# Attention and gated-MLP backward on one core: one late gradient store split 17/15/96 over the DMA engines, and small loads behind the last eight stores

## The chip, the cores and the metric

The kernel runs on one core of a Trainium2 chip. The metric is device time in microseconds (us) for one execution of the whole program; lower is better. Five engines run beside each other and wait for each other through semaphores: TensorE (PE) multiplies matrices, VectorE (DVE) and ScalarE (ACT) do elementwise work, GpSimd (POOL) and SyncE (SP) mainly start transfers here. Sixteen DMA engines move the data between HBM and the core's on-chip memory (SBUF). A transfer (a "DMA") is started by SP, by ACT or by Pool; each of the three has its own queue, and a transfer is cut into packets that are shared out over some or all of the sixteen engines. When all of a transfer's engines have finished, its completion semaphore stands 16 higher.

## The reference, cut to what matters

One decode step (one token) of a block with cached attention and a SwiGLU MLP in parallel, forward and backward:

```
xn  = layernorm(x)                                        # x: 1 x 1 x 640
q   = (xn @ wq) as 32 heads of 128                        # wq: 640 x 4096
p   = softmax(q . k_cache * 128**-0.5)                    # k_cache, v_cache: 32 heads x 8192 x 128
att = concat(p @ v_cache) @ wo                            # wo: 4096 x 640
mlp = (silu(xn @ w1) * (xn @ w3)) @ w2                    # w1, w3: 640 x 1728, w2: 1728 x 640
out = x + att + mlp
grads = vjp(out)(grad_out)   # of x, k_cache, v_cache, wq, wo, w1, w3, w2
```

All tensors are bf16. With one token, every weight gradient is an outer product: wo's gradient, for instance, is the attention output (4096 values) times grad_out (640 values). The gradients of the two caches are as large as the caches: for each head 8192 x 128 values of V's gradient (p times a row) and as many of K's. So the program reads each cache once and writes two tensors of their size: 151.34 MB in and 151.34 MB out.

## The kernel before

The program first does the MLP with its gradients, then goes head by head through the 32 heads. For each head SP loads K (2 MB) and V (2 MB). DVE multiplies them by the query and by the output gradient, PE sums, DVE and ACT build the two gradients of the head in the SBUF tile `ot`, and a store writes each out. Up to head 29 these stores go to Pool's queue, one of 2 MB each (`outer_v`, line 458). The last two heads (`TAIL = 2`) store each gradient in two halves of 1 MB from SP instead (line 456): eight stores, called s1 to s8 below, issued when DVE and ACT have finished the half.

The heads come in eight groups of four (`GH = 4`, `NG = 8`). `finish_steps` ends a group: ACT writes the group's wo gradient over the tile `wo_g` (line 374), and stores it (128 rows, one per SBUF partition, of 2560 values or 5,120 bytes). For group 6 (`g == NG - 2`) the store isn't issued there but put on the list `late` (lines 375 and 376). In head 29's turn (`h == H - 3`) the list is emptied on Pool's queue (line 787), behind Pool's last 2 MB store: wq's gradient of a pair of groups (1,280 KB), wo's gradient of group 6 (640 KB), wq's gradient of group 6 (640 KB). Behind the list stands `turn_lanes(0)`, explained next. Then, after the last head, SP stores wo's gradient of group 7 (line 827), ACT stores wq's of group 7 (`dwq_t`, line 824, forty pieces of 1,024 bytes for each DMA engine), SP stores x's gradient (`dx_bf`, line 855) and ACT stores the output (`fin_bf`, five rows of 256 bytes, line 860).

Some helpers count DMA engines, which the kernel calls lanes (`LANES = 16`). The kernel's count goes like this: a Pool transfer of 128 rows gives each engine eight rows; a Pool transfer whose number of rows has no factor of 16 goes to as many neighbouring engines as the largest factor up to 16 says (120 rows to 15 engines, 15 rows to 15, 11 rows to 11, and 17 rows, a prime, to one), starting at the engine behind the one where the last such transfer ended. `dealt[0]` holds that starting engine, and `turn_lanes(to)` moves it to `to` by loading a few rows of 32 bytes into a tile that nobody reads (`lane_pad`): k rows move it by k, and 17 rows by one. `sparing` uses this to keep 120 of 128 rows of some wq stores off engine 4 (`SPARED`). `turn_lanes(0)` at the end brings the count back to 0, with 11 rows on engines 5 to 15.

The order of instructions on each engine is the order of the program text (`manual_schedule`). The compiled program gives the transfers of SP and ACT eight completion semaphores in turn, and Pool's transfers another eight. A transfer that takes over a semaphore waits, on its issuing engine, until the transfer that had it before has landed. So each transfer of SP or ACT waits for the one eight before it in their common order.

Of the kernel before, what the change touches and what calls it, by code (L numbers as in the profile page):

```python
# [16 lines left out]
P = 128  # L17
# [4 lines left out]
def kernel(  # L22
# [22 lines left out]
    nc = tc.nc  # L45
# [23 lines left out]
    LANES = 16  # L69
# [23 lines left out]
    wq_v = A_wq.rearrange("(p ci) n -> p ci n", ci=NC)  # L93
    dwq_v = out_4.rearrange("(p ci) n -> p ci n", ci=NC)
    wo_v = A_wo.rearrange("(g p r) c -> g p r c", p=P, r=GH)
    dwo_v = out_5.rearrange("(g p r) c -> g p r c", p=P, r=GH)
# [7 lines left out]
    with tc.manual_schedule(engines=ORDERED):  # L104
# [26 lines left out]
        lane_pad = consts.tile([P, 2, 2, 8], BF16, name="lane_pad")  # L131
        dealt = [0, 0]

        def turn_lanes(to):
            k = (to - dealt[0]) % LANES
            if k:
                rows = k if k > 1 else LANES + 1
                nc.gpsimd.dma_start(lane_pad[0:rows, dealt[1] % 2], wq_v[0:rows, 0:2, 0:8])
                dealt[:] = to % LANES, dealt[1] + 1

        def deal(dst, src, p0, p1):
            nc.gpsimd.dma_start(dst[p0:p1], src[p0:p1])
            dealt[0] = (dealt[0] + (LANES - 1 if p0 == 0 else P - p0)) % LANES

        def sparing(dst, src):
            rows = P - P % (LANES - 1)
            if dealt[0] == (SPARED + 1 + P - rows) % LANES:
                deal(dst, src, rows, P)
                deal(dst, src, 0, rows)
                turn_lanes(SPARED + 1)  # L150
            else:
                turn_lanes(SPARED + 1)
                deal(dst, src, 0, rows)
                turn_lanes(SPARED + 1)
                deal(dst, src, rows, P)

        def store(dst, src, later=False, by=nc.gpsimd.dma_start):
            if later:
                late.append((by, dst, src))
            else:  # L160
                by(dst, src)
# [5 lines left out]
        def wq_part(b, c0, n):  # L167
            cols = slice(b * GW * DH, (b + 1) * GW * DH)
            return wq_two[:, c0:c0 + n, b % 2, :], wq_v[:, c0:c0 + n, cols], dwq_v[:, c0:c0 + n, cols]
# [180 lines left out]
        def on_cols(g):  # L350
            on_ps = ps_w.tile([P, GH], F32, name="on_ps", tag="w")
            for hh in range(GH):
                nc.tensor.matmul(on_ps[hh * (P // GH):(hh + 1) * (P // GH), :], lhsT=sel[:], rhs=grp[g]["om"][:, hh, :],
                                 start=True, stop=True, skip_group_check=True)
            on = small.tile([P, GH], F32, name="on")
            nc.scalar.copy(on[:], on_ps[:])
            on_bf = small.tile([P, GH], BF16, name="on_bf")
            nc.scalar.copy(on_bf[:], on[:])
            return on, on_bf
# [6 lines left out]
        def finish_steps(g):  # L366
            G_ = grp[g]
            wo_g = G_["wo"]
            on, on_bf = on_cols(g)
            behind_o.append((g, on_bf))  # L370
            yield
            assert not behind_o
            for r in range(GH):
                nc.scalar.activation(wo_g[:, r, :], g_bc_bf[:], ACTF.Copy, scale=on[:, r:r + 1])
            if g == NG - 2:
                store(dwo_v[g], wo_g[:], True)
            else:
                nc.scalar.dma_start(dwo_v[g], wo_g[:])
            yield
            yield  # L380
            b, k = divmod(g, HB)
            for ci in range(NC):
                nc.scalar.activation(G_["wq"][:, ci, :], G_["dqbc"][:].rearrange("p h d -> p (h d)"),
                                     ACTF.Copy, scale=xn_col[:, ci:ci + 1])
            if g < NG - HB and k == HB - 1:
                if g == NG - HB - 1:
                    part, _, dst = wq_part(b, 0, NC)
                    store(dst, part, True)
                else:
                    columns.extend((b, *part) for part in WQ_PARTS)  # L390
                    store_columns()
            if g >= NG - HB:
                store(dwq_v[:, :, g * GH * DH:(g + 1) * GH * DH], G_["wq"], True)
            grp.pop(g)
# [38 lines left out]
        def outer(st, vec, w2, wf, which, h, half):  # L433
            outer_v(st, vec, w2, which, h, half, outer_s(st, vec, wf, half))
# [14 lines left out]
        def outer_v(st, vec, w2, which, h, half, n):  # L449
            j0 = half * JH  # L450
            nc.vector.tensor_tensor(st.ot[half][:, 0:n],  # L451
                                    vec.rearrange("p (a b) -> p a b", b=2).unsqueeze(1).to_broadcast([P, n, DH // 2, 2]),
                                    w2[:, j0:j0 + n, :].unsqueeze(2).to_broadcast([P, n, DH // 2, 2]), ALU.mult)
            dst = {"V": dvc, "K": dkc}[which][h]
            if h >= H - TAIL:
                nc.sync.dma_start(dst[:, j0:j0 + JH, :], st.ot[half].rearrange("p j a b -> p j (a b)"))
            elif half:
                nc.gpsimd.dma_start(dst.rearrange("p j d -> p (j d)"), st.rows[:])  # L458
                if columns:
                    store_columns()  # L460
# [4 lines left out]
        def store_columns():  # L465
            b, c0, n = columns.pop(0)
            part, _, dst = wq_part(b, c0, n)
            store(dst, part, by=sparing)
# [96 lines left out]
        def keep_dq(st):  # L565
            G_, hh = st.G, st.hh
            if hh == 0:
                G_["dqbc"] = wpool.tile([P, GH, DH], BF16, name="dqbc_g", tag="dqbc_g", bufs=1)
            nc.scalar.copy(G_["dqbc"][:, hh, :], st.ps_db)
            if hh == GH - 1 and st.g < NG - 1:  # L570
                steps.append(finish_steps(st.g))
# [109 lines left out]
        for b in range(NB):  # L681
            rows, src = (P, w2t[:, b, :]) if b < NF else (REST, w2r)
# [62 lines left out]
        for h in range(H - 1):  # L745
            n = new_head(h + 1) if h + 1 < H else None
            c = hs.pop(h)
            g, hh = divmod(h, GH)
# [51 lines left out]
        g = c.g  # L800
# [33 lines left out]
        for ci in range(NC):  # L834
            k, c = divmod(ci * P, WIDE_COLS)
# [55 lines left out]
```

## Time and profile before

| | us |
|---|---|
| median of 3 runs | 718.69 (718.24 to 719.10) |
| the profiled execution, its own time | 718.87 |
| its span in the profile | 717.1 |
| granted TensorE clock, mean | 0.889 |
| busy: PE, DVE, ACT, POOL | 557.1, 630.6, 484.2, 49.5 |
| mean rate of all transfers | 423 GB/s |

The times of the runs are those of the device for one execution. The profile is of one execution: its span runs from the first to the last instruction, and 1.8 us of its own time lie outside the span. "Busy" counts computing instructions alone, so it doesn't hold the time in which an engine waits. The share of the DMA engines is the mean over the sixteen. The profile's packet records name the queue, start, duration and size of each packet, but not the DMA engine that moved it.

### The profile page before, as it was taken

What the parts mean: (1) busy time and instruction counts of PE and PEld (TensorE: products, weight loads), DVE (VectorE), ACT (ScalarE), POOL (GpSimd) and SP (SyncE); (2) the same over time, 40 slices, a digit from 0 to 9 for tenths busy, and PEclk for the clock granted to TensorE, in tenths of its full rate; (3) what the DMA queues carried; (4) which work ended last, traced back from release to release, by engine and by line L of the source; (5) the groups of instructions that cost most, each with busy time, mean ns of one, the idle gap of its engine ahead of it and who ended that gap; (6) DMA issues with size and microseconds to landing.
All of it is one profiled execution on the core that took longest, in us unless ns stands there. A gap on an engine that the chain in (4) does not pass through costs nothing.

```text
span 717.1 us, 9854 instructions
## 1 busy us (share of the span) xinstructions
PE 557.1 (78%) x3516; PEld 272.4 (38%) x3516; DVE 630.6 (88%) x723; ACT 484.2 (68%) x1472; POOL 49.5 (7%) x91
## 2 busy tenths in 40 slices
PE   6878988878788777776887787488868789877772
PEld 4753443334333333333343344143434334333331
DVE  5789999999989895997899899499999889899982
ACT  1275778796769656694587867468677857777552
POOL 0010000000001110000000110000000000000100
PEclk9698999998989998997899989899999878999995
DMA  9999999999999999999999999999999999999997
GB/s 364 416 425 430 431 430 430 429 429 429 428 432 428 426 428 424 429 427 426 432 431 428 430 422 426 428 430 429 428 428 431 429 430 431 429 430 429 429 421 288
DMA packets 27039, 303.32 MB, mean 423 GB/s; under 512 B 3249, under 2 KB 3959, under 8 KB 9327
## 3 DMA queue, kind: packets, MB, share of 16 engines
q1 hardware_dynamic: 12832, 154.88, 50.9%
q0 software_dynamic: 10960, 137.72, 45.2%
q10 hardware_dynamic: 3198, 10.10, 3.5%
q8 instruction: 27, 0.44, 0.2%
q14 instruction: 22, 0.17, 0.1%
HBM read 151.34 MB, written 151.34 MB: 422 GB/s over the span
## 4 chain that ended last, share of the span: by engine, by line
DMA 45%; DVE 31%; PE 17%; ACT 3%; issue 2%; POOL 0%; ACTq 0%; DVEq 0%; POOLq 0%
DMA Kt<-in_A_k_cache_dram 28%; DVE T L425 15%; DMA out_dram<-ot 12%; DVE ot L451 10%; PE ob L500 4%; DMA lane_pad<-in_A_wq_dram 4%; PE psS L427 3%; PE psDP L427 3%; ACT ot L445 2%; DVE DP_sb L526 1%; DVE S_sb L472 1%; PE dh_ps L591 1%; PE dx_ps L626 1%; PE gate_ps L602 1%; PE ps_od L516 1%
## 5 line engine op out<-in xcount | busy, mean ns | idle before, releaser
L427 PE MATMUL psDP<-T,ident_bf 128*128 128x512 bf16 x512 | 157.0, 462 | 64.6 <-DVE T L425 64.6
L427 PEld LDWEIGHTS <-ident_bf 128*128 128x128 bf16 x1024 | 108.3, 109 | 212.6 <-issue 140.1
L445 ACT ACTIVATE ot<-qs_g,Uf 128x128 bf16<-128x128 bf16 x504 | 154.0, 394 | 45.1 <-DVE Uf L539 27.2
L425 DVE TENSOR_TENSOR T<-Kt,qs_g 128x4096 bf16<-128x4096 bf16 x64 | 146.4, 2287 | 20.0 <-DMA Kt<-in_A_k_cache_dram 18.8
L445 ACT ACTIVATE ot<-do_g,Pf 128x128 bf16<-128x128 bf16 x512 | 156.3, 389 | 6.2 <-DMA out_dram<-ot 5.2
L425 DVE TENSOR_TENSOR T<-Vt,do_g 128x4096 bf16<-128x4096 bf16 x64 | 146.0, 2282 | 3.9 <-DMA Vt<-in_A_v_cache_dram 3.9
L427 PE MATMUL psS<-T,ident_bf 128*128 128x512 bf16 x512 | 129.0, 397 | 17.7 <-DVE T L425 17.7
L451 DVE TENSOR_TENSOR ot<-qs_g,U 128x3072 bf16<-128x3072 bf16 (+2 forms) x64 | 112.6, 1760 | 11.9 <-DMA out_dram<-ot 11.8
L451 DVE TENSOR_TENSOR ot<-do_g,P 128x3072 bf16<-128x3072 bf16 (+2 forms) x64 | 112.3, 1755 | 6.3 <-DMA out_dram<-ot 5.2
L458 POOL DMA_DIRECT2D out_dram<-ot x60 | 32.2, 537 | 549.2 <-DVE Uf L539 303.6
L500 PE MATMUL ob<-Vt,P 128*4 128x512 bf16 x512 | 64.1, 394 | 0.0
L500 PE MATMUL ob<-Kt,U 128*4 128x512 bf16 x512 | 60.5, 379 | 1.4 <-DVE U L533 1.4
L494 ACT ACTIVATE Pf<-E,rZ 128x16 f32<-128x16 f32 (+1 forms) x32 | 9.8, 307 | 60.2 <-DVE rZ L489 60.2
L558 ACT ACTIVATE dq_diag<-ident_bf,odq 128x128 bf16<-128x128 bf16 x32 | 12.8, 401 | 47.8 <-DVE odq L554 47.8
L516 PEld LDWEIGHTS ps_od<-pick,wide 128*128 128x128 f32 x256 | 38.1, 213 | 7.8 <-issue 3.0
L516 PE MATMUL ps_od<-pick,wide 128*128 128x2 f32 x256 | 33.8, 254 | 0.5 <-ACT wide L508 0.5
L500 PEld LDWEIGHTS <-U 128*4 128x4 bf16 x512 | 19.8, 84 | 37.5 <-DVE U L533 6.6
L476 PE MATMUL sm<-ident_f,mrow 128*128 128x128 f32 x64 | 15.9, 331 | 22.3 <-DVE mrow L474 22.3
L500 PEld LDWEIGHTS <-P 128*4 128x4 bf16 x512 | 20.8, 86 | 25.8 <-issue 3.5
L508 ACT COPY wide<-ob 128x256 f32<-128x256 f32 x64 | 20.1, 363 | 12.7 <-PE ob L500 12.7
L472 DVE TENSOR_REDUCE S_sb<-psS 128x64 f32<-128x512 f32 x32 | 21.9, 685 | 5.6 <-PE psS L427 5.6
L317 ACT COPY woT<-ps_t 128x512 bf16<-128x512 bf16 x40 | 22.9, 577 | 4.2 <-PE ps_t L312 3.6
(174 smaller groups left out, 552.4 us busy)
## 6 DMA issues: line engine op xcount, KB each, us to landing
out_dram<-ot POOLq DMA_DIRECT2D x60, 2048.0 KB, 24.4
Kt<-in_A_k_cache_dram SPq DMA_DIRECT2D x32, 2048.0 KB, 26.6
Vt<-in_A_v_cache_dram SPq DMA_DIRECT2D x32, 2048.0 KB, 20.0
out_dram<-ot SPq DMA_DIRECT2D x8, 1024.0 KB, 12.7
out_dram<-wo_g ACTq DMA_DIRECT2D x6, 640.0 KB, 15.1
wo_g<-in_A_wo_dram ACTq DMA_DIRECT2D x6, 640.0 KB, 15.8
wq_two<-in_A_wq_dram SPq DMA_DIRECT2D x1, 2560.0 KB, 23.8
w1t<-in_B_w_dram SPq DMA_DIRECT2D x1, 2160.0 KB
```

The costliest lines, as they stand in the source:

```text
L317: nc.scalar.copy(woT[:], ps_t[:])
L425: nc.vector.tensor_tensor(T[:], src[:, :, ds_], vec[:, ds_].unsqueeze(1).to_broadcast([P, J, DHH]), ALU.mult)
L427: nc.tensor.matmul(ps[:], lhsT=ident_bf[:], rhs=T[:, :, RUN * i:RUN * (i + 1)], start=(half == 0 and i == 0), stop=(half == 1 and i == DHH ...
L445: nc.scalar.activation(st.ot[half][:, JH - n + j].rearrange("p a b -> p (a b)"), vec, ACTF.Copy, scale=wf[:, half, j:j + 1])
L451: nc.vector.tensor_tensor(st.ot[half][:, 0:n], vec.rearrange("p (a b) -> p a b", b=2).unsqueeze(1).to_broadcast([P, n, DH // 2, 2]), w2[:, ...
L458: nc.gpsimd.dma_start(dst.rearrange("p j d -> p (j d)"), st.rows[:])
L472: nc.vector.tensor_reduce(st.S[:], st.ps["S"][:], AX.X, ALU.add)
L476: nc.tensor.matmul(st.sm[:, 8:8 + P], lhsT=mrow[:].to_broadcast([P, P]), rhs=ident_f[:], start=True, stop=True, skip_group_check=True)
L500: nc.tensor.matmul(ob[c0:c0 + WIDE, :], lhsT=w2[:, WIDE * q:WIDE * (q + 1), 0], rhs=src[:, WIDE * q:WIDE * (q + 1), :].rearrange("p j d -> ...
L508: nc.scalar.copy(part[:], ob[:, i * (WIDE // 2) * DH:(i + 1) * (WIDE // 2) * DH])
L516: nc.tensor.matmul(st.od, lhsT=st.wide[i][:, b * DH:(b + 1) * DH], rhs=pick[:, r, :], start=(r == 0), stop=(r == WIDE - 1), skip_group_che ...
L558: nc.scalar.activation(dq_diag[:], ident_bf[:], ACTF.Copy, scale=odq[:, 1:2])
```

## The change

Two things change; no arithmetic does.

First, Pool's late store of wo's gradient of group 6 becomes three stores, through the new function `more_to_last`: `turn_lanes(15)` first (10 rows, from engine 5 to engine 14), then 17 rows (one engine, by the kernel's count engine 15), 15 rows (engines 0 to 14) and 96 rows (six for each engine). By this count engine 15 moves 23 rows of 5,120 bytes where it moved 8, and each other engine 7. The final `turn_lanes(0)` now starts at engine 15, so it loads 17 rows where it loaded 11.

Second, `mark()` follows each of the eight half stores of the last two heads. It loads k rows of 16 bytes from wq into rows of `lane_pad` that nothing else uses: 17, 10, 9, 8, 7, 6 and 4 rows behind s1 to s7, and 3 and then 2 rows behind s8. They are nine loads on SP's queue.

```diff
+        def more_to_last(dst, src):
+
+            turn_lanes(LANES - 1)
+            r0 = 0
+            for k in (LANES + 1, LANES - 1, P - 2 * LANES):
+                nc.gpsimd.dma_start(dst[r0:r0 + k], src[r0:r0 + k])
+                r0 += k
+            dealt[0] = LANES - 1
+
+
+        marks = [(17,), (10,), (9,), (8,), (7,), (6,), (4,), (3, 2)]
+        marked = [24]
+
+        def mark():
+            for k in marks.pop(0):
+                nc.sync.dma_start(lane_pad[marked[0]:marked[0] + k, 0, 0], wq_v[0:k, 0, 0:8])
+                marked[0] += k
+
...
             if g == NG - 2:
-                store(dwo_v[g], wo_g[:], True)
+                store(dwo_v[g], wo_g[:], True, by=more_to_last)
...
             if h >= H - TAIL:
                 nc.sync.dma_start(dst[:, j0:j0 + JH, :], st.ot[half].rearrange("p j a b -> p j (a b)"))
+                mark()
```

In the compiled program PE, DVE and ACT have the same instructions in the same order. Pool has 3 transfers more and SP 9. Since the semaphores go round in turn, the partners of the waits change: s5, s6 and s7 now wait for s1, s2 and s3; the mark behind s7 waits for s4 to have landed; the two behind s8 wait for the mark behind s5 and for s6; the wo store of group 7 (old line 827) waits for the mark behind s6; the `dx_bf` store for s7; the `dwq_t` store for the mark behind s3, and the `fin_bf` store for s5. Before, the wo store waited for s3, the `dx_bf` store for s4, `dwq_t` for s1 and `fin_bf` for s2.

## The prediction

> **What bounds the kernel now.** I read the page's head first, then its chain of waits, then a table of windows over the last ten microseconds, then SP's waits at the end, and last the trace's packet records.
>
> ```profile
> span 717.1 us, 9854 instructions
> DMA  9999999999999999999999999999999999999997
> HBM read 151.34 MB, written 151.34 MB: 422 GB/s over the span
> DMA 45%; DVE 31%; PE 17%; ACT 3%; issue 2%; POOL 0%; ACTq 0%; DVEq 0%; POOLq 0%
> ```
>
> The sixteen DMA engines are busy in 39 of 40 slices, and transfers are the largest part of the chain. The change touches nothing before 667 us, so only the end matters. The windows there (columns: PE, PEld, DVE, ACT, POOL busy, clock, DMA share, GB/s):
>
> ```profile
> 707.00:708.00 1.00, 0.00 (x0) 0.00 (x0) 0.49 (x3) 0.00 (x0) 0.00 (x0) 0.50 1.04 414
> 709.00:710.00 1.00, 0.00 (x0) 0.00 (x0) 0.00 (x0) 0.00 (x0) 0.00 (x0) 0.50 0.74 293
> 711.00:712.00 1.00, 0.00 (x0) 0.00 (x0) 0.00 (x0) 0.00 (x0) 0.00 (x0) 0.50 0.70 261
> 713.00:714.00 1.00, 0.00 (x0) 0.00 (x0) 0.00 (x0) 0.00 (x0) 0.00 (x0) 0.50 0.31 107
> 715.00:716.00 1.00, 0.00 (x0) 0.00 (x0) 0.00 (x0) 0.00 (x0) 0.00 (x0) 0.50 0.01 1
> ```
>
> ```profile
> SPq L886 <- DMA out_dram<-ot: 5.2, 2, 2.8
> SPq L886 <- DMA out_dram<-dwq_t: 2.7, 1, 2.7
> ```
>
> Computing ends by 708 us. What is left is transfers, and SP waits for their landing at the program's end (the two waits). The DMA share falls in steps: the engines don't run out together. The last one sets the end, so the question is which engine gets the 15 extra rows.
>
> The records don't name engines, but they can be chained: a packet's successor on its engine starts 3 or 4 ns before its recorded end (of 1,157 Pool packets of 16,384 bytes after 600 us, 1,089 have a start exactly 4 ns before their end; ties are settled by the number of packets that each transfer has per engine). The last increments of the semaphores, and the last Pool load's packets, show the spread (us):
>
> ```
> dwq_t, 16 engines: 708.72 708.79 709.00 709.01 710.01 | 711.96 712.86 713.08 713.27 713.39 713.76 | 714.95 715.21 715.37 715.56 715.87
> fin_bf, engines 0-4: 709.08 710.25 713.45 715.12 716.05
> last lane_pad load, start on engines with a row (5-15): 695.34 695.45 697.17 | 702.00 702.09 702.39 702.43 702.80 | 704.68 705.59 705.69
> the five engines without a row (0-4): 693.89 695.60 703.36 706.07 706.32
> ```
>
> So five engines are early, six are in the middle, five are late, and of engines 5 to 15 three, five and three. The last of all is one of 0 to 4: `fin_bf` lands there at 716.05, and the span ends 1.05 later.
>
> Which is engine 15? The instruction queue q8 gives a handle:
>
> ```profile
> q8 instruction: 27, 0.44, 0.2%
> ```
>
> Each of its 27 packets (16 KB) holds one chained engine up for 0.86 to 0.99 us (a 16,384-byte data packet takes 0.61), and it goes round eight engines in a fixed order: the one hit at 477.9 is hit again at 689.5. All eight have a row in the last `lane_pad` load, so they are among 5 to 15. Of the five hit between 307 and 417 us, in order, the first two have no row in the 8-row store at 430 us, which the kernel deals to engines 5 to 12, and the next three have one: so I read them as 14, 15, 8, 9, 10, and the eight as 8 to 15. 27 is 3 times 8 plus 3: five of them got three fetches in the run and are the five in the middle, three got four and are the three late ones. By the order the three with four fetches are 10, 11 and 12, and 15 is a middle one, the fourth or third of its group: its `dwq_t` increment is about 713.27 (713.1 to 713.4).
>
> **The change part by part.**
>
> *17 rows on one engine.* A 5,120-byte packet starts 193 ns after the one before it on its engine (196 recorded). Engine 15 gets 23 rows for 8: 15 x 0.193 = 2.90 us. The final 17-row `lane_pad` load is a 46 ns packet of 544 bytes (as at 427.05 us) in place of a 9 ns one: 0.04. Its last landing moves from 713.27 to 716.2 (716.0 to 716.4), if it is never idle before; the DMA share is 0.98 or more until 708, and the Pool queue's rows stand far ahead of their turn: the store issued at 668.2 landed after
>
> ```profile
> out_dram<-wo_g POOLq DMA_DIRECT2D x1, 640.0 KB, 33.6
> ```
>
> *One row less on the other fifteen.* -0.193 each. Against it: an engine that has no share in a Pool transfer still moves 8 bytes per packet, as engine 4 does twelve times at 419 to 426 us in the 120-row store. 17 such packets at a pitch of 6 ns are 0.10, the dummy of the last `lane_pad` load 0.04, the extra completion packets 0.02. Sum -0.03: nothing is gained there.
>
> *Nine marks.* No 16-byte load stands in the trace. The nearest row is a 32-byte `lane_pad` packet: 9 ns, and its engine's next packet comes 6 ns later. The far row is the 1,280-byte load of x or grad_out, 55 to 89 ns. Engine 0 gets 17 + 8 rows and nine completions, 34 x 6 = 0.2 us, or at the far row 25 x 0.089 + 0.05 = 2.3; engines 1 to 4 get 5 to 8 rows, under 0.1 or at most 0.7. A gain is excluded, since they only add packets. I take 6 ns: their size is nearest to that row. Then the late ones of 0 to 4 end at 716.05 - 0.03 + 0.05 to 0.2 = 716.1 to 716.2.
>
> *SP's queue.* A mark is an issue of 0.33 us like its neighbours':
>
> ```profile
> 675.24 26.01 SPq L456 DMA_DIRECT2D out_dram<-ot  x8
> 702.11 0.41 SPq L827 DMA_DIRECT2D out_dram<-wo_g  x1
> 707.36 0.33 SPq L855 DMA_DIRECT2D out_dram<-dx_bf  x1
> ```
>
> Seven marks fall into the 2.2 to 5.5 us that SP waits for DVE between its stores. The new waits count more. s1 to s8 were issued at 675.24, 679.34, 682.24, 686.20, 692.07, 694.64, 697.20, 700.92; they landed at 687.36, 691.67, 695.66, 699.73, 703.67, 707.36, 710.69, 713.17. s5 to s7 find s1 to s3 landed (margins 4.7, 3.0 and 1.5). The mark behind s7 holds SP from 697.9 to 699.7, s8's 700.92 stands. The marks behind s8 wait for 703.7 and 707.4, so the wo store of group 7 is issued at about 707.9 for 702.11, and `dx_bf` behind s7's landing at 710.8 for 707.36. Who waits for these? Nobody but the end. On the late engines s8 itself ends only at 711.4 to 713.2, so the wo store, 1.3 us behind its issue (as `dx_bf`: issue 707.36, first packet 708.66), is there at 709.2 before they need it; the packets on ACT's queue fill the time. The early engines fall idle for up to 2 us and end near 711 for 709. Cost: 0. The cover is gone when the wo store reaches a late engine after 714.3 (its end less 8 x 0.193), that is if it is issued after 713; the margin is 5 us.
>
> *Pool's queue.* The store of group 6's wq now waits for a 2 MB store to land (673.6), the last `lane_pad` load for another (681.0). Both are needed by their engines only from 689 on: 0.
>
> **Sum.** Last landing max(716.2 on engine 15, 716.15 on 0 to 4) against 716.05: +0.15 to 0.2 on the profiled execution's own 718.87 (span 717.1 and 1.8 around it). That is 719.05; the median of the runs is 0.18 lower, so 718.9.
>
> The Trainium skill has a rule against this change: its page "DMA: Bandwidth & Descriptors", section "Latency and other measured facts", says that DMA engines 7 and 15 are usually slower than the others in traces, with a guess at Pool's descriptor rings as the cause. By it engine 15 would be late, and the time that of the first rival. The trace has the 16,384-byte packets of both queues at a median of 611 ns and lateness that follows the fetches, so I keep the rule to that rival's chance.
>
> **The rivals.**
>
> 1. Engine 15 is late. For it: the name rests on a rotation that I read from one execution; if it goes on from execution to execution, 15 gets a fourth fetch in three of eight. Against it: the 8-row store fits the rotation at five engines of five. Late ones of 5 to 15 end at 714.95 to 715.37, so with 2.94 at 717.9 to 718.3: +1.9 to 2.3 on 716.05, 720.7. It decides once engine 15's old end is over 714.5.
>
> 2. The marks cost what the far row says. For it: a load reads HBM, and x's load of 1,280 bytes is as near in kind as `lane_pad`. Against it: 32 bytes in 9 ns. It needs engine 0 to be the last one, and over 60 ns a row to show: up to +2.2, 720.9.
>
> 3. The new waits hold SP past 713. Engine 0's 17 packets take turns with Pool's, so s2 may land there 17 x 0.155 to 0.193 = 2.6 to 3.3 late, and the waits after it too; that leaves 2 of the 5 us. Beyond, each microsecond costs one: 720.
>
> 4. Faster. Engine 15 is early (ends 711.7), and an instruction fetch (0.3 us at 683.5 on a late engine of 0 to 4) falls elsewhere: 715.4, so 718.0. More than 0.2% has no route in these rows: even perfectly level ends (mean of the `dwq_t` row, 712.55) are worth 3.3.
>
> **How the numbers follow.** About 0.2% (1.4 us) is what a measurement of this kernel can tell from no change. My forecast 0.56 (own range 718.3 to 719.6); rival 1 0.26; rival 2 0.07; rival 3 0.04; rival 4 0.07, which I let stand for faster though most of it would be within. The first is "same", the next three "slower" (0.37). The range 718.2 to 721.0 takes in rival 1 and leaves out the far ends of 2 and 4.
>
> **What would show it.** Right: the 17 rows are one chain of 5,120-byte packets on one engine; that engine's `dwq_t` increment is near 716.2; the store of group 7's wo starts near 707.9; the span ends near 717.3. Wrong: an increment at 718 or later with the others where they were (rival 1); late `fin_bf` increments of two engines only (rival 2); gaps on late engines after 711 (rival 3).

## The result, and the profile after

The changed kernel took 720.43 us (median of 20 executions, 719.28 to 723.27) against 719.02 (718.24 to 721.32, 20 executions) for the kernel before on the same chip: 1.4 us more by the medians and 1.6 by the means, a ratio of 1.0023 with a 95% interval of 1.0013 to 1.0032. The forecast was 718.9, its likeliest case ended at 719.6, and the whole range at 721.0. So the time lies in the range, but on the slower side and outside the likeliest case.

The profiled execution took 719.63 (span 717.9, for 717.1 before). Its page, the same lines as before:

```profile
span 717.9 us, 9850 instructions
DMA  9999999999999999999999999999999999999997
HBM read 151.35 MB, written 151.34 MB: 422 GB/s over the span
DMA 41%; DVE 35%; PE 16%; ACT 3%; issue 2%; POOL 0%; DVEq 0%; ACTq 0%; POOLq 0%
```

The program is bound as it was: the DMA engines are full up to the last slice. The windows over the end (PE, PEld, DVE, ACT, POOL busy, clock, DMA share, GB/s), after:

```profile
707.00:708.00 1.00, 0.00 (x0) 0.00 (x0) 0.37 (x3) 0.00 (x0) 0.00 (x0) 0.50 0.98 387
709.00:710.00 1.00, 0.00 (x0) 0.00 (x0) 0.00 (x0) 0.00 (x0) 0.00 (x0) 0.50 1.00 393
711.00:712.00 1.00, 0.00 (x0) 0.00 (x0) 0.00 (x0) 0.00 (x0) 0.00 (x0) 0.50 0.84 307
713.00:714.00 1.00, 0.00 (x0) 0.00 (x0) 0.00 (x0) 0.00 (x0) 0.00 (x0) 0.50 0.65 236
715.00:716.00 1.00, 0.00 (x0) 0.00 (x0) 0.00 (x0) 0.00 (x0) 0.00 (x0) 0.50 0.12 33
```

Every window from 709 on holds more than before (at 709 a share of 1.00 for 0.74, at 713 0.65 for 0.31). That isn't one engine that runs late: a single engine is 0.06 of the share. Several engines end later. The reason shows some ten microseconds earlier, in the windows in which the rows of group 6's wo gradient are stored. The kernel before, then the changed one:

```profile
694.00:696.00 2.00, 1.10 (x12) 0.46 (x14) 1.97 (x3) 0.03 (x1) 0.00 (x0) 1.00 1.03 428
696.00:698.00 2.00, 1.53 (x15) 0.90 (x11) 1.17 (x1) 0.65 (x2) 0.00 (x0) 1.00 1.00 420
698.00:700.00 2.00, 0.87 (x14) 0.54 (x14) 1.62 (x3) 1.15 (x6) 0.00 (x0) 1.00 1.01 424
700.00:702.00 2.00, 1.02 (x8) 0.36 (x8) 2.00 (x5) 2.00 (x5) 0.00 (x0) 0.95 0.98 409
```

```profile
694.00:696.00 2.00, 1.22 (x12) 0.53 (x14) 1.97 (x3) 0.00 (x0) 0.00 (x0) 1.00 1.03 397
696.00:698.00 2.00, 1.53 (x16) 0.95 (x11) 1.05 (x1) 0.65 (x2) 0.00 (x0) 1.00 1.00 357
698.00:700.00 2.00, 0.76 (x15) 0.42 (x15) 1.73 (x3) 1.27 (x6) 0.00 (x0) 1.00 1.02 357
700.00:702.00 2.00, 1.02 (x8) 0.36 (x8) 2.00 (x6) 2.00 (x4) 0.00 (x0) 0.91 0.97 372
```

The share of busy time is the same (0.97 to 1.03), but the engines move 371 GB/s on the mean of these eight microseconds where they moved 420. Busy engines that move less have longer packets. The packet records bear it out. I call "surplus" what packets took above the usual durations (the medians of the kernel before: 611, 309, 196, 159 and 46 ns for 16,384, 8,192, 5,120, 4,096 and 1,024 bytes; the dummies of `lane_pad` loads at 46), summed over all packets of all engines that start from 684 us on (the rows name the largest parts):

```
                                      before   changed
surplus, all packets, us                 4.5      27.7
  SP's 8,192-byte packets (ot)           1.9      14.4   longest 475 -> 1,220 ns
  Pool's 5,120-byte packets (wo)         0.1       4.4   longest 229 ->   614 ns
  Pool's 4,096-byte packets (wq)         0.5       2.6   longest 441 ->   546 ns
  SP's 5,120-byte packets (wo, group 7)  0.8       2.4
  dummies of the last lane_pad load        -       2.3   median 193 ns
```

27.7 less 4.5 is 23.2 us of engine time, over sixteen engines 1.45 us each. The largest part is on packets of `ot`, which the change doesn't touch. 16.1 of the 27.7 us fall between 694 and 704 us, in which 85 of the 128 rows of group 6's wo gradient are stored; before it was 0.6 there. Not all of the rest need be the split's: 3.2 us fall after 712 us, where e3 below, which has no split, has 2.9.

The last two stores of SP's queue were issued when the forecast said. Some of SP's issues (start, length):

```profile
675.52 0.80 SPq L172 DMA_DIRECT2D lane_pad<-in_A_wq_dram  x1
704.68 3.35 SPq L172 DMA_DIRECT2D lane_pad<-in_A_wq_dram  x2
708.12 0.86 SPq L846 DMA_DIRECT2D out_dram<-wo_g  x1
710.61 0.37 SPq L874 DMA_DIRECT2D out_dram<-dx_bf  x1
```

The wo store of group 7 was issued at 708.12 (forecast 707.9) and `dx_bf` at 710.61 (forecast 710.8).

### The profile page after: what moved, and what is told of

It reads as the page before. It is cut to its first block, busy times and chain, and to the rows that moved or that the text cites. A ratio compares the mean times of both kernels' runs of the same rounds, so it can differ in the third digit from the quotient of the medians.

```text
span 717.9 us, 9850 instructions
## 1 busy us (share of the span) xinstructions
PE 553.5 (77%) x3500; PEld 272.0 (38%) x3516; DVE 630.4 (88%) x723; ACT 484.0 (67%) x1472; POOL 51.6 (7%) x94
## 4 chain that ended last, share of the span: by engine, by line
DMA 41%; DVE 35%; PE 16%; ACT 3%; issue 2%; POOL 0%; DVEq 0%; ACTq 0%; POOLq 0%
DMA Kt<-in_A_k_cache_dram 25%; DVE T L443 16%; DMA out_dram<-ot 12%; DVE ot L469 11%; PE ob L519 4%; DMA lane_pad<-in_A_wq_dram 4%; PE psS L445 3%; PE psDP L445 3%; ACT ot L463 2%; DVE DP_sb L545 1%; DVE S_sb L491 1%; PE dh_ps L610 1%; PE dx_ps L645 1%; PE gate_ps L621 1%; DVE P L510 1%
## 5 line engine op out<-in xcount | busy, mean ns | idle before, releaser
L445 PE MATMUL psDP<-T,ident_bf 128*128 128x512 bf16 x512 | 155.3, 458 | 66.9 <-DVE T L443 66.9
```

The lines of the kernel that those rows point to most:

```text
L445: nc.tensor.matmul(ps[:], lhsT=ident_bf[:], rhs=T[:, :, RUN * i:RUN * (i + 1)], start=(half == 0 and i == 0), stop=(half == 1 and i == DHH ...
```

## The experiments

Two theories stood at first. A: the split makes packets longer. B: the marks and the waits that they move cost the time. The time of each run below stands against executions of the kernel before on the same chip.

**e1: the split alone.** Edit: `more_to_last` as in the change, and no `mark()`.

```diff
-                mark()
```

> The 17/15/96 split alone, no marks. In the changed kernel's trace the packets between 684 and 718 us took 27.7 us of engine time more than their usual durations, against 4.5 us in the kernel before; the difference of 23.2 us over 16 engines is 1.45 us, the size of the slowdown of the medians (720.43 - 719.02 = 1.41). Theory A, the split stretches packets (engines read SBUF rows that lie with other engines' rows): most of the slowdown stays, +1.0 to +1.6 us, and the excess is 20 us or more. Theory B, the marks and the waits they shift: the time is that of the kernel before, within 0.4 us, excess below 8 us. Theory C, engine 15 has 15 rows too many: +1 to +2 us in those executions in which engine 15 is among the late ones, with normal packet durations.

Measured: 719.96 (719.13 to 722.49, 11 executions) against 718.87, ratio 1.0017 (1.0007 to 1.0026). Surplus 22.5 us. By this run the split alone has most of the cost and of the longer packets; its second run, e11, has 0.7 us of the 1.4.

**e2: the marks alone.** Edit: the store of group 6's wo stays whole.

```diff
-                store(dwo_v[g], wo_g[:], True, by=more_to_last)
+                store(dwo_v[g], wo_g[:], True)
```

> The nine marks alone, wo's store of group 6 whole again. Theory A: the time of the kernel before within 0.4 us, excess of packet time between 684 and 718 us below 8 us. Theory B: +1.0 to +1.6 us, excess 20 us or more or the wo store of group 7 landing last. Theory C: the time of the kernel before.

Measured: 719.24 (718.79 to 720.16), ratio 1.0002 (0.9992 to 1.0012), surplus 4.8 us. The marks alone cost nothing that shows; the interval leaves room for up to 0.9 us.

**e3: nine marks of two rows, no split.** The waits of the change without most of its small packets.

```diff
-                store(dwo_v[g], wo_g[:], True, by=more_to_last)
+                store(dwo_v[g], wo_g[:], True)
...
-        marks = [(17,), (10,), (9,), (8,), (7,), (6,), (4,), (3, 2)]
+        marks = [(2,), (2,), (2,), (2,), (2,), (2,), (2,), (2, 2)]
```

> Marks alone, nine of 2 rows each in place of 17, 10, 9, 8, 7, 6, 4, 3 and 2: same semaphores, same waits, 18 small packets in place of 66, on engines 0 and 1 alone. If the marks cost through their waits (theory B, waits): as the run with marks alone. If they cost through their packets (theory B, packets): a third of it or less. Theories A and C: the time of the kernel before within 0.4 us.

Measured: 719.40 (718.53 to 720.17), ratio 1.0005 (0.9996 to 1.0013), surplus 5.7 us. No cost of the waits can be told from zero (again up to 0.9 us are left open). Theory B falls as the main cause of the longer packets, and of the time as far as these intervals reach.

**e4: 16, 16 and 96 rows, no marks.** Three stores by blocks of rows, but no engine gets more than eight rows.

```diff
-            turn_lanes(LANES - 1)
...
-            for k in (LANES + 1, LANES - 1, P - 2 * LANES):
+            for k in (LANES, LANES, P - 2 * LANES):
```

> No marks; wo's store of group 6 in three stores of 16, 16 and 96 rows, 8 rows of 5,120 bytes for each engine as before, but not the eight neighbouring SBUF rows that an engine has in the whole store. Theory A in its first form (an engine that reads rows of another engine's part is slow): +0.5 to +1.6 us and an excess near that of the split alone. Theory A in its second form (it takes the one engine with 17 rows, or the idle shares of the other fifteen): the time of the kernel before within 0.4 us. Theory C: the time of the kernel before.

Measured: 719.28 (718.59 to 720.23), ratio 1.0005 (0.9997 to 1.0014), surplus 20.7 us. So the longer packets come without the 15 extra rows on one engine. The time is only 0.4 us longer by the medians, less than the 0.5 to 1.6 that the theory asked for, and its interval holds 1: this run shows the packets, but not their cost.

What in the split, then? Either that all engines store at the same time from only a part of the rows of `wo_g` (the 96-row store takes rows 32 to 127), or that there are three Pool transfers for one.

**e5: three stores by columns.** All 128 rows each time.

```diff
+            for r0, r1 in ((0, 1), (1, 2), (2, GH)):
+                nc.gpsimd.dma_start(dst[:, r0:r1, :], src[:, r0:r1, :])
```

> The store of wo's gradient of group 6 as three Pool transfers again, without marks, but cut by columns: all 128 rows of the first quarter (1,280 bytes a row), of the second, and of the last two (2,560 bytes a row). Each engine keeps its usual eight rows, and the number of transfers is that of the split by rows. Theory of the rows (the packets of the last 35 us get longer when sixteen engines read wo_g from only a part of the SBUF rows, as the 96-row store does): the sum of the packets' durations above their usual ones between 684 and 718 us stays below 8 us (before 4.5, split by 16, 16 and 96 rows 20.7), and the time stays within 0.4 us of the kernel before. Theory of the number of transfers (three Pool transfers in place of one set the engines against each other): the sum is 15 to 25 us, and the time 0.4 to 1.3 us longer than before.

Measured: 719.67 (718.61 to 720.90) against 719.08, ratio 1.0003 (0.9994 to 1.0011), surplus 4.3 us. The two medians are 0.6 apart, where 0.4 was expected at most, the means 0.4. The windows of this run hold the old rate (first four columns as above, last two share and GB/s):

```profile
696.00:698.00 2.00, 1.53 (x16) 0.66 (x10) 1.52 (x1) 0.65 (x2) 0.00 (x0) 1.00 1.01 421
698.00:700.00 2.00, 1.22 (x17) 0.88 (x17) 1.27 (x3) 0.85 (x3) 0.00 (x0) 1.00 1.03 429
```

Three transfers don't lengthen packets. The number of transfers is ruled out as the cause of the longer packets.

**e6: two stores of 64 rows.**

```diff
+            for r0 in (0, P // 2):
+                nc.gpsimd.dma_start(dst[r0:r0 + P // 2], src[r0:r0 + P // 2])
```

> The same store as two Pool transfers of 64 rows each, without marks: rows 0 to 63, then 64 to 127, four rows on each engine in each. Theory of the rows: all sixteen engines read first from one half of the SBUF rows and then from the other, so the sum of the packets' durations above their usual ones between 684 and 718 us is at least the 20.7 us of the split by 16, 16 and 96 rows, and the time is 0.4 to 1.6 us longer than before. The Trainium skill's page 'SBUF - State Buffer', section on door 1 (the DMA port swizzle), says that rows 0 to 63 reach only one half of sixteen ports and rows 64 to 127 only the other; by that rule this split is the worst of the cuts by rows. Theory of the number of transfers: two in place of one disturb less than three, so the sum is below 20 us, and the time within 0.5 us of before.

Measured: 720.27 (719.08 to 721.01) against 719.08, ratio 1.0011 (1.0003 to 1.0020), surplus 15.3 us. The surplus is there, with only two transfers, but it isn't the largest, as I had expected: the expectation is missed in that point.

```profile
696.00:698.00 2.00, 1.53 (x14) 0.60 (x11) 1.67 (x1) 0.65 (x2) 0.00 (x0) 1.00 1.04 408
698.00:700.00 2.00, 1.32 (x19) 1.03 (x18) 1.11 (x3) 0.84 (x3) 0.00 (x0) 1.00 0.98 373
```

**e7: the 17 rows on engine 10.** Edit: `turn_lanes(10)` and `dealt[0] = 10` in the split without marks.

> The split by 17, 15 and 96 rows without marks, with the 17 rows on engine 10 in place of engine 15. In the trace of the kernel before, engine 10 has four instruction fetches and is one of the last three of engines 5 to 15, with its last landing at 714.95 to 715.37. If the engine that takes the 15 extra rows matters as the prediction's arithmetic has it, engine 10 now lands last, 2.9 us later, at 717.9 to 718.3: 1.9 to 2.3 us longer than before from that alone, and with the longer packets of the split about 2.5 to 3.5 us longer. If the engine doesn't matter (the longer packets are all of the cost, and the fetches fall on other engines from execution to execution), the time is that of the split on engine 15, 1.1 us longer than before.

Measured: 719.29 (719.00 to 720.88), ratio 1.0008 (0.9999 to 1.0017), surplus 19.3 us. The 2.5 to 3.5 us didn't come. But engine 10 wasn't one of the late ones in the profiled execution. Of the five engines that an instruction fetch held up between 306 and 418 us, the first three have a row in the 8-row store at 430 us (engines 5 to 12) and the last two have none; in the kernel before, and in the changed one, the first two had none and the last three had one. So the rotation doesn't start at the same engine in every execution. The eleven times fall into seven of 719.00 to 719.60 and four of 719.97 to 720.88, as they would if engine 10 were late in some executions and not in others. That is a reading, not shown for each execution.

**e8: the same counts, with rows from all over the tile.** 17 rows 0, 4, ..., 64 on engine 15, 15 rows 68, ..., 124, and the other 96 as three stores of every fourth row; no marks.

```diff
+            cut = (LANES + 1) * 4
+            for a, b, d in ((0, cut, 4), (cut, P, 4), (1, P, 4), (2, P, 4), (3, P, 4)):
+                nc.gpsimd.dma_start(dst[a:b:d], src[a:b:d])
```

> As the split by 17, 15 and 96 rows without marks, the 17 again on engine 15, but with every store's rows taken from all over the tile: 17 rows 0, 4, ..., 64, then 15 rows 68, 72, ..., 124, then three stores of 32 rows (1, 5, ...; 2, 6, ...; 3, 7, ...). Theory of the rows: no part of the SBUF rows is read by all engines at once, so the sum of the packets' durations above their usual ones between 684 and 718 us falls from 22.5 (rows in blocks) to under 8 us, and the time is 0.5 to 1.4 us shorter than the split in blocks of the same call, within 0.5 us of the kernel before. If uneven rows are not the cause (small stores, or engine 15's extra rows by themselves), the sum stays at 15 to 25 us and the time with the split in blocks.

Measured: 719.20 (718.62 to 720.20) against 718.96, ratio 1.0004 (0.9996 to 1.0013), surplus 5.5 us, with the split in blocks on the same chip (e11) at 719.67. The rate is the old one, with five Pool transfers and 23 rows on engine 15:

```profile
698.00:700.00 2.00, 1.53 (x15) 0.77 (x11) 1.37 (x1) 0.65 (x2) 0.00 (x0) 1.00 1.03 421
700.00:702.00 2.00, 1.07 (x16) 0.73 (x15) 1.41 (x3) 0.98 (x4) 1.02 (x1) 1.00 1.01 422
```

The packets' half of the expectation holds clearly. The gain in time (0.5 us by the medians, 0.3 by the means) is at its lower edge or below it, and the intervals of e8 and e11 overlap, so that these two runs alone don't show it.

**e9: the same, with the 17 rows on engine 1.** Edit to e8: `turn_lanes(1)` and `dealt[0] = 1`.

> The same rows from all over the tile, with the 17 rows on engine 1, which was one of the last engines in the three traces with marks (its last mark at 711.2 to 712.6 us, engine 0's at 708 to 709). If the prediction's arithmetic for the engine that takes the extra rows is right, and only the engine's place was misread, engine 1 now lands last, 15 x 0.193 = 2.9 us later than 716.0: the time is 2.4 to 3.1 us longer than the strided split on engine 15. If the other engines or the order of the queue take the extra rows up, or the extra rows don't decide, the two are within 0.6 us of each other.

Measured: 719.31 (718.76 to 721.02), ratio 1.0011 (1.0002 to 1.0019), surplus 6.5 us. By the medians the two are 0.1 us apart, by the means 0.4. Here too the times fall apart, six of 718.76 to 719.31 and five of 719.75 to 721.02, and in the profiled one (718.99) all five held-up engines have a row in the 8-row store, a third position of the rotation. The run doesn't settle what 15 more rows cost on an engine that is late in each execution, since I found none that is.

**e10 and e12: the whole change, marks and all, with the rows of e8.**

> The whole change, marks and all, with the rows of the three parts taken from all over the tile (17, 15 and three times 32). If the longer packets are all of the change's cost, the sum above the usual durations is under 8 us and the time within 0.6 us of the kernel before, where the change itself took 1.4 us more. If marks and waits cost something together with the split, the time stays 0.6 to 1.6 us above the kernel before.

> The whole change with rows from all over the tile once more, because the first profile of it was of its slowest execution (721.0 us, 14.6 us of packet time above the usual durations). If that execution was an exception, the time is again within 0.6 us of the kernel before and a profile of an execution near the median has less than 10 us above the usual durations between 684 and 718 us. If the marks lengthen packets when they run beside the split, the profile has 12 us or more whatever its time, and the theory of the rows explains only a part of the change.

Measured: e10 719.34 (718.67 to 721.00) against 718.96, ratio 1.0001 (0.9992 to 1.0010), surplus 14.6 us in its slowest execution. e12 719.78 (719.00 to 721.65, 12 executions) against 718.89, ratio 1.0013 (1.0004 to 1.0022), surplus 8.7 us in an execution at the median. The first met its time, not its surplus; the second its surplus, not its time. Their mean ratio, 1.0007, lies between the kernel before and the change (1.0023). So with spread rows the surplus above the kernel before falls from 23.2 us to 10.1 and 4.2, and the cost, by the mean ratio, to less than half; but e12's interval overlaps that of the change, and up to 0.9 us may be left that the packets don't explain.

**e11: the split in blocks once more.**

> The split in blocks of 17, 15 and 96 rows without marks once more, for the comparison on the same chip in the same call: by its first runs 0.7 to 1.9 us longer than the kernel before, with 17 to 27 us of packet time above the usual durations.

Measured: 719.67 (718.99 to 720.04) against 718.96, ratio 1.0010 (1.0001 to 1.0019), surplus 23.3 us; the time is right at the expectation's lower edge.

```profile
694.00:696.00 2.00, 0.75 (x8) 0.35 (x10) 1.97 (x3) 0.48 (x1) 0.00 (x0) 1.00 1.04 378
696.00:698.00 2.00, 1.53 (x16) 0.65 (x10) 1.52 (x1) 0.65 (x2) 0.00 (x0) 1.00 0.99 379
698.00:700.00 2.00, 1.22 (x17) 0.88 (x17) 1.26 (x3) 0.85 (x3) 0.00 (x0) 1.00 1.01 374
```

e8 and e11 differ in which rows go together (and so in the number of stores, which e5 cleared): 421 GB/s between 698 and 700 us for 374.

What none of these runs can separate is the two ends of the store. Row p of `wo_g` goes to row p of the gradient in HBM, 5,120 bytes behind row p-1, so a block of SBUF rows is also one block of HBM addresses, and rows at a stride, or columns, are spread at both ends. Whether the engines hinder each other in SBUF or in HBM stays open.

**The traces laid side by side.** The span is the packets' time plus the engines' idle time, both per engine (packet durations, each less the 4 ns, or 3 for the smallest, by which it overlaps its successor, summed and divided by 16; what is left of the span is idle). The last two columns are the surplus of all packets, summed over the engines, before and from 684 us on:

```
us                       span   packets/16  idle/16   surplus <684  >684
before                  717.10    709.85      7.24        48.0       4.5
marks alone (e2)        717.05    710.50      6.55        59.6       4.8
columns (e5)            716.84    709.77      7.06        49.7       4.3
changed                 717.86    711.27      6.59        50.2      27.7
blocks (e1)             718.69    711.78      6.91        65.0      22.5
blocks again (e11)      717.22    710.88      6.34        48.2      23.3
spread, no marks (e8)   718.43    711.72      6.71        80.5       5.5
spread, marks (e10)     719.23    711.13      8.10        59.6      14.6
spread, marks (e12)     718.01    710.28      7.73        53.2       8.7
```

Two things can be read here. The changed kernel's packets take 1.42 us more per engine than before, about its surplus; the idle time is 0.65 less, and so this execution's span grew by 0.77. That some of the longer packets fell on engines that had ended early would explain the 0.65; it isn't shown. And a single span says little: e8's is long because its surplus before 684 us, where its program is the one before, happened to be 80 for 48 (2 us per engine). That is the scatter of single executions, and why the ratios above rest on many.

In those ratios the groups lie closer together than in the surplus. The five cuts by blocks without marks (e1, e4, e6, e7, e11) have 1.0005 to 1.0017, on the mean 1.0010; the five runs without blocks that have either the marks or another cut (e2, e3, e5, e8, e9) have 1.0002 to 1.0011, on the mean 1.0005, each with an interval of about 0.0009 to both sides. So it is shown that blocks of rows lengthen packets. That this is the whole 1.4 us isn't.

## Why the prediction was right and wrong

That the time lies inside the stated range was luck: the range reached up to 721.0 for the sake of the first rival, a late engine 15, and that isn't what happened. The forecast itself was 1.5 us too low, and its sum had no term for what the runs show.

**The failing step is "One row less on the other fifteen ... nothing is gained there", and under it the price of 0.193 us a row.** I counted packets and multiplied by the durations that they had in the kernel before, as if a packet's duration belonged to its size alone. Here it also depended on how a store beside it was cut into rows. Cutting the tile by blocks of rows made the wo packets longer (mean 230 ns for 197), and even more those of other stores beside them. The term that I set at -0.03 us measured +1.45 per engine in packet time, 1.0 of it between 694 and 704 us. In device time e1 and e11 put the split at 1.1 and 0.7 of the 1.4 us; the remainder has no shown cause. e1, e4, e6, e7 and e11 show it in five traces (15 to 23 us of surplus), e5 and e8 show that it goes away when each store takes rows from all of the tile. No rival of mine had it.

A rule of the Trainium skill speaks of this, and I had not weighed it. Its page "DMA: Bandwidth & Descriptors", section "The descriptor swizzle", says that in a transfer of 128 rows into SBUF each engine writes the eight rows of one SBUF port; the page "SBUF — State Buffer", section on door 1 (the DMA port swizzle), says that rows 0 to 63 reach one half of sixteen ports and rows 64 to 127 the other. If stores out of SBUF are dealt the same way, a whole store, or one by columns, would keep the engines apart, and a block of rows would send engines to each other's ports. Neither page gives a price for what runs beside such a store, and the traces agree in part: blocks lengthen packets, columns and spread rows don't. They disagree on the order: by the second rule 64-row halves (e6) should be the worst cut, and they have the smallest surplus of the cuts by blocks (15.3 us for 19.3 to 23.3). That ports are the cause isn't shown by these runs, nor that the cause lies in SBUF at all.

**Engine 15 a middle one: wrong.** The chaining of packets holds: of the 1,157 Pool packets that the prediction counts, 1,155 have a start 3 or 4 ns before their end (1,058 exactly 4, not 1,089). The naming of the engines didn't. The final `lane_pad` load of 17 rows has one packet of 544 bytes, on engine 15. It came at 695.29 in the changed kernel (694.18 in e11, 696.53 in e1), second or third of the sixteen engines, though it stands behind the 15 extra rows in Pool's queue; in the kernel before, the middle engines had their row at 702.0 to 702.8 and the early ones at 695.3 to 697.2. Engine 15 is an early one, and by the order of the fetches it has none; the two held-up engines without a row in the 8-row store were then 13 and 14, not 14 and 15, and the eight go from 7 to 14. So its 15 rows (+2.9 us) didn't make it the last engine, and my 716.2 for it was a wrong term that happened not to matter. No engine's `dwq_t` increment came at 718 or later (the last at 716.57). That the 17 rows are one chain on one engine wasn't shown; the single packet of the 17-row load speaks for it. The first rival (engine 15 late) falls with it. Its 720.7 is near the measured time, but not by its mechanism. The premise of the fourth (engine 15 early, so faster) was true, and the time still rose. The Trainium skill's rule that engines 7 and 15 are usually slower (page "DMA: Bandwidth & Descriptors", section "Latency and other measured facts") isn't borne out for 15 here.

**The marks: right.** Of the 66 packets of 16 bytes 65 took 9 ns, and e2 and e3 show no cost that can be told from zero. The second rival falls. The 17 rows on engine 0 did take turns with Pool's packets at the start, as the third rival feared, 13 of them 0.16 us apart, but SP's last two stores were still issued within 0.2 us of the forecast.

**SP's and Pool's waits: right.** Both SP stores started within 0.2 us of the forecast, Pool's waits ended at 673.8 and 681.2 (forecast 673.6 and 681.0), and the last landing is that of `dwq_t` (716.57), not of a delayed store (`dx_bf`: 716.40). What I had wrong is the length of the marks' issues: 0.8 to 1.8 us each behind s1 to s7 for the 0.33 forecast. SP had the time. The third rival falls.

**The sum.** Forecast +0.15 to 0.2 on the span's last landing; the profiled execution has +0.77, the median of all executions +1.4. My likeliest case was a time that can't be told from the kernel before; the three slower cases (0.37 together) had the direction, but no case had the cause.

**Still open.** Whether the marks add something once the split is there: e10 and e12 differ (ratios 1.0001 and 1.0013), and in both the idle time is higher than before (8.10 and 7.73 for 7.24), while Pool's store of group 6's wq is issued at 689 to 690 us for 673.8, since two more stores stand before it. And what makes two of the engines 0 to 4 late (three in the changed kernel, whose `fin_bf` increments come at 715.96 to 716.36): by the order of the fetches, those on q8 don't hit them.

## What to carry to other kernels

When a store is cut into pieces, ask which rows each piece covers, not only how many packets an engine gets: pieces by columns, or rows from all over the tile, left the rate at 419 to 425 GB/s (404 in e10, one of the two runs that also had the marks), blocks of rows took it to means of 371 to 401 for eight microseconds, also for transfers beside them. In these windows, a full DMA share with fewer GB/s was the sign of it. And before work is dealt to one engine by name, find that engine in the trace by something only it moves, and in more than one execution: here the late ones among eight changed from execution to execution, while one (engine 15) was early each time that it could be seen.

## What the runs showed that I had not expected

- A packet of 8,192 bytes, 309 ns as a rule, took up to 1,220 ns while other engines stored blocks of rows of another tile.
- The rotation of instruction fetches over eight engines (27 fetches, recorded at 0.88 to 1.07 us, where the prediction has 0.86 to 0.99) had three different positions in five executions, so which three of the eight engines get a fourth fetch isn't fixed.
- A load of 4 to 17 rows of 16 bytes took SP 0.8 to 1.8 us to issue beside the split, and 0.35 to 0.95 us in e2 without it (the first seven marks), where a 1 MB store took 0.35 in e2. In e10 and e12, with the rows spread, seven loads took 0.27 to 1.42, so the block cut alone isn't the reason.
- On engines without a share, thirteen of the fifteen dummies of a 17-row load took 94 to 424 ns late in the changed kernel; those of the kernel before took 46 ns at 428 to 430 us.
